# Windowed attention and a PReLU feed-forward layer in one kernel: weights converted earlier, and the first tile's activation split over two slots

## The chip, the cores and the metric

The kernel runs on one core of one Trainium2 chip. The metric is device time in microseconds (us) of one execution; a kernel is run several times and the median counts. Profiles are of single executions taken by the hardware profiler. Engines are named as in the profile: PE multiplies matrices (PEld is its loading of weights), DVE is the vector engine, ACT the scalar (activation) engine, SP the engine that issues the transfers.

## The reference

Inputs are q, k and v of shape (8, 8, 576, 64) (batch, head, position, head dimension), two matrices w_in (512 x 2048) and w_out (2048 x 512), and a vector alpha of 2048. Cut to what matters:

```python
scores = q @ k.T / sqrt(64)          # per batch and head
# heads 0-3: the last 32 positions; heads 4-7: every 4th of the last 128
attn = softmax(where(mask, scores, -1e9))
x = (attn @ v)                       # laid out as 4608 tokens x 512
h = x @ w_in
g = maximum(h, 0) + alpha * minimum(h, 0)
out = g @ w_out
```

## The kernel before, in words

**Work and tiles.** Attention is cut into units `Unit(b, c, u)`: batch b, head pair c (4), half u (2) of the 576 positions; 8 units a batch, 64 in all. A unit has these steps: `load` (L106, issued by SP), `scores` on PE (L124, tile `s`), `maxima` on DVE (L139, mask and row maximum), `exponentials` on ACT (L148), `divisions` on DVE (L155 to L158), `transposes` on PE (L165, tile `t`), `copies` on ACT (L170, tile `pt`), `values` on PE (L177, tile `o`), and `highs` on ACT (L210) and `lows` on DVE (L214), which write the result to `x` as two parts, a rounded high part and the rest. All products of the feed-forward layer are made from such pairs, as three passes (high x high, high x low, low x high).

The feed-forward layer takes the 4608 tokens in 9 tiles of 512 (t) and the 2048 hidden columns in 16 chunks of 128 (f). One (t, f) is a slot here, numbered n = 16 t + f. A slot has `ffn_h` (L259, 12 matmuls into a PSUM tile `h`), `ffn_g` (L264 to L279: PReLU to `m`, then the cast of its high part to `g`, L277), `ffn_low` (L283, low part of `g`), and `ffn_y` (L291, 12 matmuls that add into four PSUM tiles `y`). In the first tile (`begin`) the PReLU goes over ACT: relu of -h to `m` (L269), relu of h to `r` (L270), and one sum on DVE (L271). In the other tiles it is two instructions on DVE (L274, L275).

**Weights.** w_in and w_out arrive as 64-bit floats, in 32 chunks of 512 KB: `load_weight(which, f)` stages one in a buffer of tag "g" (SP, L223 or L225), `convert_weight` makes 32-bit high and low parts of it: an Abs on ACT (L238), four integer and clamping steps on DVE (L239, L240, L242, L244; tile `wa`, tag "m"), a cast on ACT (L246) and a subtraction on DVE (L247). A chunk (0, f) of w_in is needed by h of hidden chunk f, a chunk (1, f) of w_out by y of it. The converted weights stay in SBUF for the other eight tiles.

**Order.** `wq` lists the chunks in the order of their need. Before the first slot comes a loop over 11 steps, which runs the 8 units of batch 0 as a pipeline: scores of unit s, divisions of unit s-1, transposes of s-2, values of s-3. At its steps 3, 5, 7 and 9 it converts one chunk and loads the next; two chunks are staged ahead. Then slots 0 to 143 follow. While `wq` holds chunks, a slot converts two of them, one behind `exponentials` and one behind `lows`: 28 chunks in slots 0 to 13. Batch 1's units start in slots 0, 2, 4, 6, 8, 10, 12 and 13 (scores there, transposes a slot later, values two slots later), so that two slots share one unit. `pending` delays y: by one slot in the first tile, by two later.

**Buffers.** Pool `ffp` has 4 buffers of tag "g" (the two parts of g; staged chunks) and 4 of tag "m" (`m`, `r`, `wa`, the output). PSUM has 4 banks of tag "a" (s, t, o and h) and 4 of tag "y" (y; before the first slot, s of batch 0). `early` is a third room of the x pool and holds the probabilities of batch 0.

**What sets the order on an engine.** The text of the kernel gives priorities. The framework turns it into one fixed list of instructions for each engine, in which an instruction may stand ahead of others that the text has earlier, and adds the waits. On the chip each engine works its list in order.

## Time and profile before

| | us |
|---|---|
| median of 3 runs | 994.12 |
| lowest, highest | 988.69, 994.39 |
| the profiled execution | 995.82 |
| its span, first to last instruction | 993.9 |
| PE, DVE, ACT busy in the span | 964.2, 580.9, 382.9 |

The busy time of an engine is the time in which it has an instruction under way; matmuls are pipelined and their ends are modelled, so a PE that is busy all the time isn't at its peak. PEclk is the clock granted to PE, as tenths or as a share of full speed. In groups a row reads: line, engine, operation, output<-input, count | busy us, mean ns of one | idle time of the engine ahead of it and what ended it. In a list of waits: the engine and line that waited, for whom, us in total, times, longest. In a timeline: start, length, engine, line, operation, count, and in brackets the idle time ahead of it. In a table of stages: from:to, length, then busy us (and instructions) of PE, PEld, DVE, ACT, POOL, then the granted clock, the share of DMA time and GB/s.

### The profile page before, as it was taken

How to read it: one execution, taken by the hardware profiler on the slowest of the kernel's cores; microseconds unless marked ns; L12 is line 12 of the kernel's file. 1: busy time of each engine (PE TensorE's matmuls, PEld its weight loads, DVE VectorE, ACT ScalarE, POOL GpSimd, SP SyncE). 2: the span in 40 equal slices, each digit the busy share in tenths (PEclk: the TensorE clock that was granted, in tenths of full speed). 3: DMA queues.
4: the chain of work that ended last, by engine and by line, in shares of the span. 5: the costliest groups of instructions: out<-in, count | busy, mean ns of one | idle time of the engine just before them, and what ended most of it. 6: DMA issues, size and time to landing. Idle time of an engine off the chain costs nothing.

```text
span 993.9 us, 14724 instructions
## 1 busy us (share of the span) xinstructions
PE 964.2 (97%) x5388; PEld 770.4 (78%) x5388; DVE 580.9 (58%) x1732; ACT 382.9 (39%) x1267; POOL 0.6 (0%) x6
## 2 busy tenths in 40 slices
PE   7699999999999999999999999999999999999998
PEld 4466766788888888888888888888888888888886
DVE  5869899755555556655555556555555544434343
ACT  5757667533433334433343334333433321111111
POOL 0000000000000000000000000000000000000000
PEclk8579899999999999999999999999999999999999
DMA  7334543211112111211121112111121001001001
GB/s 234 116 104 163 164 156 125 83 41 40 41 38 67 33 41 40 83 41 41 41 82 36 32 41 83 41 41 40 41 74 32 1 1 43 1 1 43 0 1 43
DMA packets 39303, 58.78 MB, mean 59 GB/s; under 512 B 3808, under 2 KB 28480, under 8 KB 39232
## 3 DMA queue, kind: packets, MB, share of 16 engines
q1 hardware_dynamic: 39232, 57.84, 18.6%
q8 instruction: 43, 0.70, 0.3%
q14 instruction: 28, 0.23, 0.1%
HBM read 48.39 MB, written 9.44 MB: 58 GB/s over the span
## 4 chain that ended last, share of the span: by engine, by line
PE 88%; DVE 7%; ACT 2%; issue 1%; DMA 1%; SPq 0%; ACTq 0%
PE h L259 38%; PE y L291 37%; PE s L124 5%; PE o L177 4%; PE t L165 3%; DVE wa L244 1%; DVE wa L242 1%; DVE wa L239 1%; DMA q<-qT 1%; DVE pr L139 1%; ACT early L148 1%; DVE wi L247 1%; DVE pr L158 1%; DVE wo L247 1%; DVE m L271 1%
## 5 line engine op out<-in xcount | busy, mean ns | idle before, releaser
L291 PE MATMUL y<-g,wo 128*128 128x512 f32 x1728 | 431.1, 397 | 7.2 <-ACT g L277 7.2
L259 PE MATMUL h<-x,wi 128*128 128x512 f32 x1728 | 427.4, 397 | 0.0
L259 PEld LDWEIGHTS h<-x,wi 128*128 128x128 f32 x1728 | 331.2, 192 | 69.8 <-issue 0.4
L291 PEld LDWEIGHTS y<-g,wo 128*128 128x128 f32 x1728 | 315.8, 188 | 81.4 <-ACT g L277 10.6
L274 DVE TENSOR_SCALAR m<-h,al 128x512 f32<-128x512 f32 x128 | 96.1, 751 | 278.8 <-PE h L259 274.2
L277 ACT CAST g<-m 128x512 fp32r<-128x512 f32 x144 | 89.5, 621 | 188.5 <-DVE m L275 185.8
L283 DVE TENSOR_TENSOR g<-m,g 128x512 fp32r<-128x512 f32 x144 | 99.1, 688 | 55.8 <-ACT g L277 55.6
L148 ACT ACTIVATE pr<-pr,nm 96x128 f32<-96x128 f32 x336 | 130.8, 392 | 2.3 <-DVE nm L139 2.2
L210 ACT CAST x<-o 128x288 fp32r<-128x288 f32 (+8 forms) x112 | 36.0, 393 | 218.3 <-PE o L177 218.3
L170 ACT COPY pt<-t 128x288 f32<-128x288 f32 x128 | 46.2, 400 | 141.7 <-PE t L165 141.2
L275 DVE SCALAR_TENSOR_TENSOR m<-h,m 128x512 f32<-128x512 f32 x128 | 88.5, 692 | 4.4
L139 DVE CUSTOM_DVE_ANT_0 pr<-s,mask_sb 96x128 f32<-96x128 f32 x336 | 75.2, 281 | 0.0
L124 PE MATMUL s<-k,q 64*96 64x128 f32 x768 | 62.2, 290 | 5.1 <-DMA q<-qT 5.1
L148 ACT ACTIVATION_READ_ACCUMULATOR pr<-pr,nm 96x1 f32 x336 | 63.6, 189 | 0.0
L158 DVE TENSOR_TENSOR pr<-pr,rs 96x384 f32<-96x384 f32 x112 | 57.7, 550 | 1.7
L124 PEld LDWEIGHTS s<-k,q 64*96 64x96 f32 x768 | 47.1, 165 | 14.8 <-issue 6.7
L177 PEld LDWEIGHTS o<-pt,v 128*64 128x64 f32 x768 | 37.2, 143 | 23.9 <-issue 20.5
L177 PE MATMUL o<-pt,v 128*64 128x96 f32 x768 | 50.9, 264 | 0.6 <-ACT pt L170 0.2
L165 PEld LDWEIGHTS t<-ident,pr 96*128 96x128 f32 x336 | 34.4, 142 | 15.2 <-DVE pr L158 8.1
L165 PE MATMUL t<-ident,pr 96*128 96x96 f32 x336 | 40.2, 252 | 4.2 <-DVE pr L158 4.1
L214 DVE TENSOR_TENSOR x<-o,x 128x288 fp32r<-128x288 f32 (+8 forms) x112 | 41.4, 383 | 3.7 <-ACT x L210 3.7
L139 DVE DVE_READ_ACCUMULATOR2_ANT nm<- 96x1 f32 x384 | 30.4, 79 | 0.0
(33 smaller groups left out, 281.6 us busy)
## 6 DMA issues: line engine op xcount, KB each, us to landing
v<-vW SPq DMA_DIRECT2D x64, 192.0 KB, 2.3
k<-kT SPq DMA_DIRECT2D x32, 288.0 KB, 3.2
q<-qT SPq DMA_DIRECT2D x64, 144.0 KB, 2.8
out<-ob SPq DMA_DIRECT2D x36, 256.0 KB, 2.2
ws<-w_in SPq DMA_DIRECT2D x16, 512.0 KB, 3.6
ws<-w_out SPq DMA_DIRECT2D x16, 512.0 KB, 3.5
mask_sb<-masks SPq DMA_DIRECT2D x1, 144.0 KB, 3.6
al<-alpha SPq DMA_DIRECT2D x1, 8.0 KB, 3.2
```

Of the source, the lines that this page charges most:

```text
L124: nc.tensor.matmul(self.ps[e][:, i, :], lhsT=self.q[rows, i * BQ:(i + 1) * BQ], rhs=self.k[rows, self.starts[j]:self.starts[j] + P], start ...
L139: nc.vector.tensor_tensor_reduce(out=self.pr[e][:, i, :], in0=self.ps[e][:, i, :], in1=mask_sb[:, self.kinds[j], :], scale=-SCALE, scalar= ...
L148: nc.scalar.activation(out=self.pr[e][:, i, :], in_=self.pr[e][:, i, :], func=AF.Exp, bias=self.nm[:, e, i:i + 1], scale=-1.0, accum_out=s ...
L158: nc.vector.tensor_tensor(out=self.pr[e], in0=self.pr[e], in1=rs[:, e, :, None].broadcast_to([BQ, UB, P]), op=ALU.mult)
L165: nc.tensor.transpose(out=self.tp[e][:, i, :], in_=self.pr[e][:, i, :], identity=ident)
L177: nc.tensor.matmul(self.po[e * D:(e + 1) * D, i, :], lhsT=self.v[:, e, i, :], rhs=self.pt[e][:, i, :], start=True, stop=True,)
L259: nc.tensor.matmul(ps, lhsT=wi[:, a, f, c, :], rhs=x[:, c, e, :], start=(n == 0), stop=(n == 3 * NC - 1))
L274: nc.vector.tensor_scalar(out=m, in0=ps, scalar1=0.0, scalar2=al[:, f:f + 1], op0=ALU.min, op1=ALU.mult)
L275: nc.vector.scalar_tensor_tensor(out=m, in0=ps, scalar=0.0, in1=m, op0=ALU.max, op1=ALU.add)
L277: nc.scalar.copy(out=g[:, 0, :], in_=m)
L283: nc.vector.tensor_tensor(out=g[:, 1, :], in0=ms.pop((t, f)), in1=g[:, 0, :].bitcast(F32), op=ALU.subtract)
L291: nc.tensor.matmul(ys[t][c], lhsT=wo[:, a, f, c * P:(c + 1) * P], rhs=g[:, e, :], start=(f == 0 and n == 0), stop=(f == NF - 1 and n == 2),)
```

## The change

The order of `wq` stays. Four things are edited:

- A function `weight()` converts the next chunk and loads one more. The attention loop calls it at steps 1 to 8, behind `exponentials` and ahead of `lows` and `divisions`, instead of at steps 3, 5, 7 and 9 behind `divisions`. So 8 chunks stand ahead of the first slot and 24 are left for slots 0 to 11.
- Three chunks are loaded ahead of the loop instead of two: the first behind the masks and ahead of the second unit's q and v, the second behind those, the third behind alpha.
- In the first tile `ffn_g` is split. `ffn_relu` issues the two relus, the second now in place in the PSUM tile of h (no tile `r`), late in the slot. `ffn_sum` does the sum and the cast at the head of the next slot, reading the relu of h from PSUM. The first `weight()` of a slot stands right behind that, ahead of `maxima`; `ffn_low`, at its old place, is that of the slot before; the second `weight()` stands behind the relus. y keeps its slot: y of slot n is still issued at the end of slot n+1.
- The other tiles do what they did; the first slot of the second tile also does the sum, cast and low of the last slot of the first.

```diff
-    def ffn_g(t, f, spare_dve):
+    def ffn_relu(t, f):
+
         ps = ms[t, f]
         m = ffp.tile([P, TT], F32, tag="m", name=f"m_{t}_{f}")
-        if spare_dve:
-            r = ffp.tile([P, TT], F32, tag="m", name=f"r_{t}_{f}")
-            nc.scalar.activation(out=m, in_=ps, func=AF.Relu, scale=-1.0)
-            nc.scalar.activation(out=r, in_=ps, func=AF.Relu)
-            nc.vector.scalar_tensor_tensor(
-                out=m, in0=m, scalar=nal[:, f:f + 1], in1=r, op0=ALU.mult, op1=ALU.add)
...
+        nc.scalar.activation(out=m, in_=ps, func=AF.Relu, scale=-1.0)
+        nc.scalar.activation(out=ps, in_=ps, func=AF.Relu)
+        ms[t, f] = ps, m
+
+    def ffn_sum(t, f):
+        ps, m = ms[t, f]
+        nc.vector.scalar_tensor_tensor(
+            out=m, in0=m, scalar=nal[:, f:f + 1], in1=ps, op0=ALU.mult, op1=ALU.add)
+        gs[t, f] = g = ffp.tile([P, 2, TT], F32R, tag="g", name=f"g_{t}_{f}")
+        nc.scalar.copy(out=g[:, 0, :], in_=m)
+        ms[t, f] = m
...
+    loads = list(wq)
+
+    def weight():
+        if wq:
+            convert_weight(*wq.pop(0))
+            if loads:
+                load_weight(*loads.pop(0))
+
...
     nc.sync.dma_start(out=mask_sb, in_=masks)
+    load_weight(*loads.pop(0))
     first[1].load()
+    load_weight(*loads.pop(0))
     nc.sync.dma_start(out=al, in_=alpha)
     nc.vector.tensor_scalar_mul(nal, al, -1.0)
-    loads = list(wq)
-    load_weight(*loads.pop(0))
     load_weight(*loads.pop(0))
...
             u.exponentials()
+        if 1 <= s <= len(first):
+            weight()
         if u := at(3):
             u.lows()
         if u := at(1):
             u.divisions()
-        if s >= 3 and s % 2 and ahead:
-            convert_weight(*wq.pop(0))
-            load_weight(*loads.pop(0))
-            ahead -= 1
...
-        ffn_g(t, f, begin)
+
+        if begin:
+            done = raw
+            for args in done:
+                ffn_sum(*args)
+            weight()
+        else:
+            done = raw + [(t, f)]
+            for args in raw:
+                ffn_sum(*args)
+            ffn_g(t, f)
         for u in score:
             u.maxima()
         for u in value:
             u.highs()
         for u in score:
             u.exponentials()
-        if wq:
-            convert_weight(*wq.pop(0))
-            if loads:
-                load_weight(*loads.pop(0))
-        ffn_low(t, f)
+        for args in done:
+            ffn_low(*args)
         for u in value:
             u.lows()
-        if wq:
-            convert_weight(*wq.pop(0))
-            if loads:
-                load_weight(*loads.pop(0))
+        raw = []
+        if begin:
+            ffn_relu(t, f)
+            raw = [(t, f)]
+            weight()
         for u in score:
             u.divisions()
-        while len(pending) >= lag:
+        if begin:
+            pending += done
+        while len(pending) >= (1 if begin else 2):
             ffn_y(*pending.pop(0))
-        pending.append((t, f))
+        if not begin:
+            pending += done
```

More of the change, by code (lines that the diff above doesn't have):

```diff
@@ L262, in ffn_h, with ffn_g @@
         ms[t, f] = ps
-    def ffn_g(t, f, spare_dve):
+    def ffn_relu(t, f):
         ps = ms[t, f]
         m = ffp.tile([P, TT], F32, tag="m", name=f"m_{t}_{f}")
-        if spare_dve:
-            r = ffp.tile([P, TT], F32, tag="m", name=f"r_{t}_{f}")
-            nc.scalar.activation(out=m, in_=ps, func=AF.Relu, scale=-1.0)
-            nc.scalar.activation(out=r, in_=ps, func=AF.Relu)
-            nc.vector.scalar_tensor_tensor(
-                out=m, in0=m, scalar=nal[:, f:f + 1], in1=r, op0=ALU.mult, op1=ALU.add)
-        else:
-            nc.vector.tensor_scalar(out=m, in0=ps, scalar1=0.0, scalar2=al[:, f:f + 1], op0=ALU.min, op1=ALU.mult)
-            nc.vector.scalar_tensor_tensor(out=m, in0=ps, scalar=0.0, in1=m, op0=ALU.max, op1=ALU.add)
+        nc.scalar.activation(out=m, in_=ps, func=AF.Relu, scale=-1.0)
[8 more added lines that the diff above has]
+        ms[t, f] = m
+    def ffn_g(t, f):
+        ps = ms[t, f]
+        m = ffp.tile([P, TT], F32, tag="m", name=f"m_{t}_{f}")
+        nc.vector.tensor_scalar(out=m, in0=ps, scalar1=0.0, scalar2=al[:, f:f + 1], op0=ALU.min, op1=ALU.mult)
+        nc.vector.scalar_tensor_tensor(out=m, in0=ps, scalar=0.0, in1=m, op0=ALU.max, op1=ALU.add)
         g = ffp.tile([P, 2, TT], F32R, tag="g", name=f"g_{t}_{f}")
@@ L306, in tile_window_attention_prelu_ffn @@
     wq = [(0, 0), (0, 1), (1, 0), (0, 2)]
-    ahead = len(wq)
     for f in range(1, NF):
@@ L368, in tile_window_attention_prelu_ffn @@
             todo[s + 2][3].append(unit)
-    pending = []
+    pending, raw = [], []
     for n in range(NTILE * NF):
@@ L373, in tile_window_attention_prelu_ffn @@
         begin = t == 0
-        lag = 1 if begin else 2
         load, score, trans, value = todo[n]
```

## The prediction

> **What bounds the kernel now.** I read the page's slices first, then a table of stages, then who waited for whom on the engine that came out full.
>
> ```profile
> span 993.9 us, 14724 instructions
> PE   7699999999999999999999999999999999999998
> DVE  5869899755555556655555556555555544434343
> ACT  5757667533433334433343334333433321111111
> PEclk8579899999999999999999999999999999999999
> ```
>
> A slice is 24.8 us. From the ninth on, PE is full at full clock and DVE has a third of its time free: there the change touches nothing that could matter. Only the first eight slices, some 190 us, have gaps on PE, and there DVE is at 8 or 9 tenths. The same stretch as a table of stages (busy us on each engine, then granted clock and DMA share):
>
> ```profile
> 7.80:53.40 45.60, 32.43 (x237) 23.87 (x234) 34.20 (x162) 32.40 (x134) 0.00 (x0) 0.64 0.50 160
> 53.40:74.20 20.80, 18.49 (x90) 13.38 (x90) 15.15 (x41) 12.22 (x31) 0.00 (x0) 0.80 0.34 110
> 74.20:158.50 84.30, 77.34 (x399) 58.63 (x398) 78.63 (x213) 57.71 (x155) 0.00 (x0) 0.92 0.50 160
> 158.50:177.00 18.50, 16.45 (x93) 12.16 (x92) 18.24 (x58) 13.75 (x43) 0.00 (x0) 1.00 0.27 91
> 116.80:133.40 16.60, 15.29 (x81) 11.57 (x79) 15.32 (x44) 10.76 (x31) 0.00 (x0) 0.91 0.45 146
> 206.40:219.60 13.20, 13.20 (x80) 10.67 (x79) 7.18 (x23) 4.72 (x19) 0.00 (x0) 1.00 0.14 39
> ```
>
> The first row is the attention of batch 0 with four chunks of weights, up to the start of the first tile's work; the next three hold the other 28 chunks, two a slot. The fifth is one pair of slots out of that stage (two slots share one attention unit): DVE and PE each work 15.3 of 16.6 us. The last is a pair of the next tile, which PE alone sets at 13.2 us. So conversions cost: a pair with four of them takes 16.6 us where PE needs 13.2. The last chunk ends at 177:
>
> ```profile
> L247 DVE TENSOR_TENSOR wo<-wa,wo x1: 681/681/681, 176.3 to 176.3; 128x512 fp32r<-128x512 f32 x1
> ```
>
> From 7.8 to there DVE works 34.20 + 15.15 + 78.63 + 18.24 = 146.2 us and idles 45.6 + 20.8 + 84.3 + 18.5 - 146.2 = 23.0 us. Where that idle time lies (waits of DVE from 7 to 60 us, then from 60 to 177):
>
> ```profile
> DVE early L139 <- PE s L124: 5.3, 4, 2.9
> DVE x L214 <- ACT x L210: 3.7, 2, 2.6
> DVE m L271 <- ACT r L270: 3.3, 1, 3.3
> DVE wi L247 <- ACT wi L246: 2.2, 1, 2.2
> DVE wa L239 <- ACT wa L238: 0.7, 2, 0.4
> ...
> DVE m L271 <- ACT r L270: 5.3, 5, 2.3
> DVE wi L247 <- ACT wi L246: 2.5, 6, 0.6
> ```
>
> The two waits for r, 8.6 us together, are what the delayed sum aims at; 5.3 us are maxima waiting for scores, 3.7 us the last lows before the first h.
>
> **The change, part by part.** No computing instruction is removed or added: 32 conversions, the same relus, sums, casts and lows. What moves is which work DVE may do while it would idle. So the sum is one of DVE's idle time.
>
> *The price of a conversion.* A group's mean is longer than what an instruction takes from DVE, since neighbours overlap; starts count (start, length):
>
> ```profile
> 100.12 0.68 DVE L247 TENSOR_TENSOR wi<-wa,wi 128x512 fp32r<-128x512 f32 x1
> 100.72 0.68 DVE L242 SCALAR_TENSOR_TENSOR wa<-ws,wa 128x512 uint32<-128x512 uint32 x1
> 101.32 0.42 DVE L239 TENSOR_SCALAR wa<-wa 128x512 f32<-128x512 f32 x1
> 101.66 0.68 DVE L244 SCALAR_TENSOR_TENSOR wa<-ws,wa 128x512 uint32<-128x512 uint32 x1
> 102.26 0.42 DVE L240 TENSOR_SCALAR wa<-wa 128x512 uint32<-128x512 uint32 x1
> ```
>
> L247, L242 and L244 take 0.60 us, L239 and L240 0.34: 2.48 us a chunk. The rows are also out of the text's order (L242 between another chunk's steps): each engine's instructions stand in an order made from the text, not in the text's own, so a chunk that has landed can be taken into a gap.
>
> *Eight chunks instead of four ahead of the first h.* That puts 4 x 2.48 = 9.9 us on DVE into the first row's 45.6 us, which has 11.4 free, and takes two slots' worth of conversions off the end: the last chunk falls in slot 11, not 13. Work before the last chunk then drops by what slots 12 and 13 hold besides conversions, 15.32 - 9.92 = 5.4 us. The last chunk ends at 7.8 + 146.2 - 5.4 + I = 148.6 + I, I being DVE's idle time up to there. Two more slots are then to be done at PE's pace, 13.2 us, before the position of 177 is reached. So the change saves 177 - (148.6 + I + 13.2) = 15.2 - I. It pays only if I falls well below the present 23.0; 7.8 us of the idle time removed only pay for what moved.
>
> *I in the attention stage* (11.4 now). The 5.3 us before scores are time in which a landed chunk can be converted. But one chunk is now issued ahead of the second unit's loads and three ahead of the third's. Its q already lands late behind two chunks (start and length):
>
> ```profile
> 5.59 7.64 DMA q<-qT
> ...
> ws<-w_in SPq DMA_DIRECT2D x4, 512.0 KB, 5.3
> q<-qT SPq DMA_DIRECT2D x12, 144.0 KB, 3.2
> ```
>
> Against a median of 3.2 us it takes 7.64, so two chunks cost some 4.4 us and the third 2.2. SP issues in order, so the key, q and v loads behind it move too. I take 2 us left of 5.3 (bounds 0 and 5.3 + 2.2). The lows' 3.7 us can be filled by chunks 9 and 10, if staged: 1.5 left (0 to 3.7). Waits of a chunk's last step for ACT's cast and of its first for ACT's Abs are 2.9 us with four chunks; eight in the same stretch, on an ACT that is busy 32.4 of 45.6 us and gets another 4 x (Abs + cast): 3.5 (1 to 5.8). Sum 7.
>
> *I from the first h to slot 3* (5.65 now). The sum of slot n stands at the head of slot n+1, so the 3.3 and 2.3 us of waiting for r go. What is late next is the relu behind h(0), for which ACT holds its queue, the next Abs among it. I take 1 (0 to 2.3).
>
> *I in the six pairs of slots 0 to 11* (74.2 to 158.5: 84.3 - 78.63 = 5.7 us over five pairs, 1.1 a pair). DVE needs 15.3 and PE, as it runs there, 15.3 too:
>
> ```profile
> 133.13 0.47 PE L165 MATMUL t<-ident,pr 96*128 96x96 f32 x3 [0.60 <-DVE pr L158]
> 133.38 4.58 PE L259 MATMUL h<-x,wi 128*128 128x512 f32 x12
> 141.31 2.88 PE L259 MATMUL h<-x,wi 128*128 128x512 f32 x12
> 144.03 2.88 PE L291 MATMUL y<-g,wo 128*128 128x512 f32 x12
> ```
>
> The h behind the transposes takes 4.58 us, the other 2.88, like y: after waits of under a us the clock is down (0.91 in that pair). The transposes still wait for the divisions and h still stands behind them. Two engines that need 15.3 each and hang on each other do not reach 15.3; I take 0.7 of idle time a pair, 4.2 (bounds 0.3 and 1.1, the present value: 1.8 to 6.7).
>
> The Trainium skill, "TensorE: Matmul & The Clock Gate", Part 1 (The HAM clock gate), says that the clock halves only after an idle window of about 3.4 us. The trace differs: here it drops with waits below 1 us. By the rule PE would need only 13.2 a pair, DVE alone would be the limit, the pairs' idle time would go to its lower bound and the result would be about 2 us faster than by the rows; I go by the rows.
>
> *The relu in place and the sum from PSUM.* No row shows ACT writing 512 wide into PSUM. The nearest are these (mean ns):
>
> ```profile
> L271 DVE SCALAR_TENSOR_TENSOR m<-m,nal,r 128x512 f32<-128x512 f32 x11 | 8.2, 746 | 5.3 <-ACT r L270 5.3
> L275 DVE SCALAR_TENSOR_TENSOR m<-h,m 128x512 f32<-128x512 f32 x128 | 88.5, 692 | 4.4
> ```
>
> The second already reads one input from PSUM and is 54 ns shorter; over the 11 sums before the last chunk 0.6 us, between 0 and 0.6. ACT has a third of its time free in the tile stage, so a relu dearer or cheaper by a tenth of a us is hidden; without that cover 16 of them cost 1.6.
>
> *Three chunks staged instead of two.* They hold three of the four "g" buffers. It removes waits of ACT for landings:
>
> ```profile
> ACT wa L238 <- DMA ws<-w_in: 5.0, 4, 1.7
> ```
>
> These four waits hide behind DVE's own backlog (DVE waited 0.3 us for an Abs after 60 us): 0. The price on g is the second rival.
>
> *Sum.* I = 7 + 1 + 4.2 = 12.2; saving 15.2 - 12.2 + 0.6 = 3.6 us. The profiled execution took 995.82 us with a span of 993.9; 995.8 - 3.6 = 992.2. The median shown, 994.12, lies 1.7 below that execution, so the forecast for the median is 990.5. The terms' bounds give I from 1 + 0 + 1.8 = 2.8 to 17 + 2.3 + 6.7 = 26, that is 12.4 + 0.6 saved to 10.8 lost, 981 to 1005; the likeliest case is the middle of this, 984 to 999.
>
> **Rivals.**
>
> *DVE's idle time all but goes* (I of 2.8 to 5). For it: every large wait of DVE's list is of a kind that an early chunk or the delayed sum can cover. Against: PE's own 15.3 a pair at the lowered clock, and that covering needs the instruction order to fit real durations. Saving 10.8 to 13, middle 12: 982.
>
> *One g buffer becomes the bound; slower.* With three of four held by staged chunks, the cast of slot n+1 must wait until y of slot n has left its buffer. Per slot: cast, low, y, and on PE, which works in order, an h and half a unit's products. With the rows
>
> ```profile
> L277 ACT CAST g<-m 128x512 fp32r<-128x512 f32 x144 | 89.5, 621 | 188.5 <-DVE m L275 185.8
> L283 DVE TENSOR_TENSOR g<-m,g 128x512 fp32r<-128x512 f32 x144 | 99.1, 688 | 55.8 <-ACT g L277 55.6
> ```
>
> that is 0.62 + 0.69 + 2.88 + 2.88 to 4.58 for h + about 1.1 = 8.2 to 9.9 us, against DVE's 7.7 a slot. It decides once PE runs an h between a low and its y: then a pair takes 16.4 to 19.7 us, middle 18, DVE idles 2.7 a pair, I = 8 + 6 x 2.7 = 24.2, 15.2 - 24.2 + 0.6 = 8.4 lost: 1002.5. Behind a held cast on ACT stand the next Abs and exps, for which DVE waits. Against it: y can be put ahead of that h, which leaves 5.3 us, and the order is free to do so.
>
> *The change doesn't do what it says*: the early chunks land too late (5.3 us median, DMA share 0.5 in the stage) or stand too late in the engines' order, conversions run as now, and only the waits for r go: but they only become the wait for h. Then the last chunk stays near 177, and the time near 994. For it: in the present trace the chunks already run whenever there is room.
>
> **How the numbers follow.** Chances: the forecast 0.52, idle time gone 0.23, one g buffer 0.14, nothing moved 0.11. The predicted time is the forecast's, 990.5. A measurement of this kernel can tell about 1%, 9.9 us: below 984.2 or above 1004.1. Faster takes most of the first rival and a little of the forecast's edge, 0.25; slower most of the second, 0.12; within 1% the rest, 0.63. The range, 981 to 1003, is the span of the terms' bounds, cut to the second rival's middle.
>
> **What would show it.** Right: eight L247 end before the first h's end, the last chunk ends near 160, waits of the sum for a relu below 1 us in all, DVE busy 15.3 of about 16 us a pair, six such pairs and then 13.2 us. The first h, whose present last matmuls are these,
>
> ```profile
> 51.29 4.28 PE L259 MATMUL h<-x,wi 128*128 128x512 f32 x10
> ```
>
> should end later than at 55.6, by 1 to 8 us. Wrong: the last chunk after 170; L277 waiting for "PE y" in most slots of the first tile; scores of the third unit waiting over 5 us more for q; or any difference behind 200 us, where nothing is changed.

## The result and the profile after

The changed kernel takes 998.0 us, median of ten runs (996.71 to 1000.12); the kernel before, run beside it, 988.6 us, median of ten (987.0 to 994.39). The ratio is 1.008, interval 1.0057 to 1.0103: 9.4 us slower, where 3.6 us faster was forecast. The time lies inside the predicted range, but on the other side of the kernel before.

The kernel before needs a word of its own, since everything is measured against it. Its 130 runs in the sessions of this study lie between 984.7 and 996.4 us, 49 of them below 990 and 73 above 991. The clock granted to PE goes with the time: of the 120 runs that were timed beside the experiments, the 43 below 990 us have 0.979 to 0.986, the 69 above 991 us 0.972 to 0.979. The execution that was shown ahead of the prediction, 995.82 us, is one of the long ones. The changed kernel's runs do not spread like that. Against the median of all 130, 992.0, the changed kernel loses 6.0 us; against that of its own session, 9.4.

The page of the changed kernel, its span and slices (24.9 us each):

```profile
span 997.8 us, 14728 instructions
PE   7669899999999999999999999999999999999998
DVE  6879998655555555555555556555555544334343
PEclk7569999999999999999999999999999999999999
```

DVE stands a tenth lower in the seventh and eighth slice: the conversions do end earlier. But the third slice of PE, from 50 to 75 us, is at 6 where it was at 9, and the clock is a tenth lower in the first and the third. As stages (busy us and instructions on PE, PE's weight loads, DVE, ACT, POOL; granted clock, DMA share, GB/s):

```profile
7.80:53.40 45.60, 29.86 (x198) 22.75 (x198) 39.58 (x171) 35.27 (x135) 0.00 (x0) 0.57 0.64 209
53.40:74.20 20.80, 14.31 (x71) 9.96 (x70) 14.21 (x44) 10.61 (x31) 0.00 (x0) 0.66 0.26 84
74.20:158.50 84.30, 76.66 (x411) 58.06 (x410) 79.05 (x212) 56.98 (x151) 0.00 (x0) 0.95 0.47 150
158.50:177.00 18.50, 18.19 (x120) 14.08 (x119) 12.99 (x46) 11.90 (x40) 0.00 (x0) 1.00 0.15 43
```

In the first row DVE does more than before (39.58 us for 34.20), as planned, but PE does less (198 matmuls for 237): the attention of batch 0 has fallen behind. In the second row the first h, which ended at 55.6 before, ends only at 66.0, and DVE is busy for only 14.21 of 20.8 us. The fourth is what was wanted, PE nearly alone. The last chunk and the waits of DVE from 60 to 190 us:

```profile
L247 DVE TENSOR_TENSOR wo<-wa,wo x2: 683/684/686, 158.4 to 162.6; 128x512 fp32r<-128x512 f32 x2
```

```profile
DVE m L274 <- ACT h L269: 12.7, 7, 4.2
DVE x L214 <- ACT x L210: 3.1, 2, 2.7
```

The last chunk ends at 163.3 (before: 177). The sum still waits for a relu: what was a wait for r is now a wait for the relu in place (tile h, L269). Of the 12.7 us, 4.8 lie ahead of the end of the last chunk; the rest lies where PE is full and DVE's idle time costs nothing. The prediction's sign was below 1 us. The first h's last matmuls and the first y:

```profile
62.13 3.85 PE L259 MATMUL h<-x,wi 128*128 128x512 f32 x10
...
73.60 0.79 PE L300 MATMUL y<-g,wo 128*128 128x512 f32 x1 [3.84 <-ACT g L277]
```

The first h ends at 66.0, not at 55.6. The end of the 17th h, the first of the next tile, is at 189.4 (before: 185.3), and from there to the span's end it is 808.4 us here and 808.6 before. So the whole difference lies ahead of 190 us, where it was looked for.

### The profile page after: what moved, and what is told of

Its sections match the earlier page's. It is cut to its first block, busy times and chain, and to the rows that moved or that the text cites. A ratio compares the mean times of both kernels' runs of the same rounds, so it can differ in the third digit from the quotient of the medians.

```text
span 997.8 us, 14728 instructions
## 1 busy us (share of the span) xinstructions
PE 962.3 (96%) x5388; PEld 770.2 (77%) x5388; DVE 581.6 (58%) x1732; ACT 382.6 (38%) x1267; POOL 0.6 (0%) x6
## 4 chain that ended last, share of the span: by engine, by line
PE 90%; DVE 3%; ACT 3%; DMA 2%; issue 1%; SPq 0%; ACTq 0%
PE y L300 40%; PE h L259 38%; PE s L124 4%; PE o L177 4%; PE t L165 3%; DMA ws<-w_out 1%; ACT pr L148 1%; DMA q<-qT 1%; ACT wa L238 1%; ACT early L148 0%; DVE wa L242 0%; DVE early L158 0%; DVE m L274 0%; DVE wa L244 0%; ACT m L268 0%
## 5 line engine op out<-in xcount | busy, mean ns | idle before, releaser
L259 PE MATMUL h<-x,wi 128*128 128x512 f32 x1728 | 421.5, 392 | 1.7 <-DVE m L274 1.5
L259 PEld LDWEIGHTS h<-x,wi 128*128 128x128 f32 x1728 | 325.3, 189 | 70.6 <-DVE m L274 2.1
L283 DVE TENSOR_SCALAR m<-h,al 128x512 f32<-128x512 f32 x128 | 96.1, 751 | 279.5 <-PE h L259 274.9
L286 ACT CAST g<-m 128x512 fp32r<-128x512 f32 x128 | 79.5, 621 | 186.5 <-DVE m L284 185.9
L292 DVE TENSOR_TENSOR g<-m,g 128x512 fp32r<-128x512 f32 x144 | 99.0, 688 | 55.8 <-ACT g L286 55.6
L139 DVE CUSTOM_DVE_ANT_0 pr<-s,mask_sb 96x128 f32<-96x128 f32 x336 | 75.0, 281 | 0.0
L177 PE MATMUL o<-pt,v 128*64 128x96 f32 x768 | 53.5, 270 | 0.7 <-ACT pt L170 0.5
L139 DVE DVE_READ_ACCUMULATOR2_ANT nm<- 96x1 f32 x384 | 30.2, 79 | 0.0
```

The source lines that it names most:

```text
L139: nc.vector.tensor_tensor_reduce(out=self.pr[e][:, i, :], in0=self.ps[e][:, i, :], in1=mask_sb[:, self.kinds[j], :], scale=-SCALE, scalar= ...
L177: nc.tensor.matmul(self.po[e * D:(e + 1) * D, i, :], lhsT=self.v[:, e, i, :], rhs=self.pt[e][:, i, :], start=True, stop=True,)
L259: nc.tensor.matmul(ps, lhsT=wi[:, a, f, c, :], rhs=x[:, c, e, :], start=(n == 0), stop=(n == 3 * NC - 1))
L283: nc.vector.tensor_scalar(out=m, in0=ps, scalar1=0.0, scalar2=al[:, f:f + 1], op0=ALU.min, op1=ALU.mult)
L286: nc.scalar.copy(out=g[:, 0, :], in_=m)
L292: nc.vector.tensor_tensor(out=g[:, 1, :], in0=ms.pop((t, f)), in1=g[:, 0, :].bitcast(F32), op=ALU.subtract)
```

## The experiments

After the result there were two theories. One: the attention stage of batch 0 has no DVE time to give; what is put there delays the first h by as much, and a chunk costs more there than in the slots. The rival: the loss comes from the slots of the first tile (here the tile stage), from the delayed sum, the relus in place, or from windows of lowered clock. A third reading, that DVE's total work is the bound so that any work taken off it helps, came in on the way. The table gives, of each profiled run, the end of the first h, the end of the 17th, and the span; behind the 17th h all have 808.3 to 809.4 us left.

| kernel | first h | 17th h | span |
|---|---|---|---|
| before, as shown | 55.6 | 185.3 | 993.9 |
| before, second execution | 53.9 | 176.2 | 984.8 |
| the change | 66.0 | 189.4 | 997.8 |
| the change, second execution | 66.3 | 189.8 | 998.2 |
| e1, weights only | 63.6 | 192.3 | 1000.6 |
| e2, relus only | 54.4 | 180.4 | 988.8 |
| e3, chunk behind the divisions | 61.7 | 187.9 | 996.3 |
| e5, two chunks ahead | 52.5 | 180.2 | 988.8 |
| e6, six ahead | 60.7 | 184.2 | 992.6 |
| e6 again | 56.3 | 179.8 | 988.2 |
| e7, three staged | 57.2 | 190.4 | 999.2 |
| e8, light chunks | 57.1 | 180.4 | 988.8 |
| e9, last step on POOL | 52.8 | 185.3 | 993.7 |
| e10, the change, last step on POOL | 61.8 | 188.3 | 996.7 |
| e11, relu in place only | 54.2 | 179.2 | 988.0 |
| e12, two ahead, last step on POOL | 48.7 | 180.3 | 989.6 |
| e13, PE filled in batch 1 | 54.2 | 184.4 | 993.5 |
| e14, PE filled in batches 0 and 1 | 52.0 | 179.3 | 987.7 |
| e15, two ahead and PE filled | 46.6 | 175.3 | 983.8 |
| e16, the change, PE filled | 65.2 | 189.6 | 998.0 |

One profile is one execution, and the kernel before shows how far two of them can be apart (9.1 us), so the verdicts on times rest on the medians. Each ratio is to the kernel before in the same session, whose median went from 988.6 to 993.7 us between sessions.

### The change in halves

The weights' half alone: the kernel before with the loads ahead of the first scores and a chunk in each of the steps 1 to 8; its slots and its relus stay.

```
+    load_weight(*loads.pop(0))
     first[1].load()
+    load_weight(*loads.pop(0))
...
+        if 1 <= s <= len(first):
+            weight()
...
-        if s >= 3 and s % 2 and ahead:
-            convert_weight(*wq.pop(0))
-            load_weight(*loads.pop(0))
-            ahead -= 1
```

> The early weights alone (three chunks staged, eight converted in the attention loop), with the activation of the first tile as before. Theory A: the loss arises in the attention stage, where eight chunks on DVE and the waits of a fixed order put the first h 10 us later, and the tile stage gives only some of it back. Then the first h ends near 66 us and the time is as slow as with the whole change, 996 to 999. Theory B (rival): the split of the activation costs the tile stage (the bank of h and the g buffer are held longer), and without it the 9.9 us of the four chunks that left the tile stage come back in full: 987 to 991.

Measured: 1001.94 us (999.1 to 1003.5, six runs), ratio 1.0116, interval 1.0083 to 1.0148, to 989.76 before: 12.2 us slower, no less than the whole change. In its profile the first h ends at 63.6, and from there to the 17th h it takes 192.3 - 63.6 = 128.7 us, where the change takes 123.4.

The relus' half alone: weights as before, relu in place directly behind h, sum a slot later.

```
+        nc.scalar.activation(out=m, in_=ps, func=AF.Relu, scale=-1.0)
+        nc.scalar.activation(out=ps, in_=ps, func=AF.Relu)
+        ms[t, f] = ps, m
...
+            done = raw
+            for args in done:
+                ffn_sum(*args)
+            weight()
```

> The split activation alone, with the weights as before (two chunks staged, four converted in the attention loop, 28 in slots 0 to 13). Theory A: the first h ends near 55.6 us as before, the tile stage is as long or 1 to 3 us shorter: 985 to 989. Theory B: the tile stage becomes longer by 4 to 8 us although nothing moved in the attention stage: 992 to 997.

Measured: 992.89 us (989.77 to 995.88, twelve runs), ratio 1.0033 (1.001 to 1.0056): 3.1 us slower. So neither half brings what it was meant to, and the larger loss comes with the weights.

To see which part of the relus' half costs, e11 has only the relu in place, without the delay:

```
-            r = ffp.tile([P, TT], F32, tag="m", name=f"r_{t}_{f}")
...
-            nc.scalar.activation(out=r, in_=ps, func=AF.Relu)
+            nc.scalar.activation(out=ps, in_=ps, func=AF.Relu)
```

> The kernel before with the second relu written in place into the PSUM tile of h (no r), the sum in the same slot and nothing delayed. It parts the two halves of the split activation, which alone made it 0.33% slower. If holding the bank of h until the sum is what costs: 992 to 994, as with the split alone. If the delay by a slot costs (cast and y of the first slots come later, PE waits and its clock falls): no difference from before, within 0.2%.

Measured: 994.02 us (989.88 to 996.59), ratio 1.0008 (0.999 to 1.0025). No difference: the relu in place and reading the sum from PSUM cost and bring nothing that can be measured. That leaves the delay, and the new order around it, for what e2 loses; but the two intervals overlap, so this is not shown.

### The kernel before, once more

> The kernel before, unchanged, for a second profile: its runs lie in two groups, near 988 and near 994, and the profile at hand is of the later group. Both theories: the two groups part in the first 190 us; a run near 988 has its last conversion 5 to 6 us ahead of 177, or its first h ahead of 55.6.

One execution, 986.75 us, span 984.8. Its stretches from the start of work to the first h's end, on to the last chunk's end, and on to the 17th h's end; first in the execution that the prediction was read from:

```profile
7.80:55.60 47.80, 34.63 (x244) 25.34 (x242) 34.25 (x162) 32.40 (x134) 0.00 (x0) 0.64 0.48 153
55.60:177.00 121.40, 110.07 (x572) 82.69 (x573) 111.97 (x309) 83.68 (x225) 0.00 (x0) 0.92 0.45 144
177.00:185.30 8.30, 8.30 (x55) 6.39 (x55) 5.06 (x22) 4.61 (x17) 0.00 (x0) 1.00 0.16 44
```

then in the second execution:

```profile
7.80:53.90 46.10, 33.72 (x246) 24.83 (x244) 34.26 (x162) 32.29 (x134) 0.00 (x0) 0.67 0.51 161
53.90:167.90 114.00, 101.19 (x572) 75.85 (x573) 111.36 (x309) 82.99 (x225) 0.00 (x0) 1.00 0.48 153
167.90:176.20 8.30, 8.30 (x55) 6.40 (x55) 5.06 (x22) 4.61 (x17) 0.00 (x0) 1.00 0.16 42
```

then in the changed kernel:

```profile
7.80:66.00 58.20, 39.80 (x242) 29.51 (x244) 46.73 (x188) 38.67 (x144) 0.00 (x0) 0.56 0.59 191
66.00:163.30 97.30, 85.83 (x473) 64.91 (x474) 90.88 (x245) 67.30 (x179) 0.00 (x0) 0.95 0.42 134
163.30:189.40 26.10, 25.79 (x155) 20.34 (x154) 14.55 (x61) 14.67 (x54) 0.00 (x0) 1.00 0.16 44
```

These nine rows are the heart of the case. The two executions of the kernel before run the same instructions (309 on DVE and 572 on PE in the second stretch), yet the second stretch takes 121.4 us in one and 114.0 in the other; DVE idles 121.40 - 111.97 = 9.4 us in the first and 114.00 - 111.36 = 2.6 in the second. The clock is 0.92 and 1.00. The waits of DVE for r in that stretch, shown execution, then the second one:

```profile
DVE m L271 <- ACT r L270: 8.6, 6, 3.3
```

```profile
DVE m L271 <- ACT r L270: 2.0, 1, 2.0
```

So most of the 8.6 us that the delayed sum was to win is absent in the execution whose clock stays up. That it goes with h at half clock is read from these two executions. The windows of half clock in the shown execution:

```profile
113.07:116.48 3.41, 1.80 (x9) 1.05 (x9) 3.08 (x8) 2.23 (x4) 0.00 (x0) 1.00 0.44 142
116.48:119.89 3.41, 3.41 (x10) 2.77 (x11) 3.38 (x8) 1.28 (x4) 0.00 (x0) 0.50 0.44 151
130.13:133.54 3.41, 2.10 (x12) 1.37 (x12) 3.41 (x10) 1.75 (x5) 0.00 (x0) 1.00 0.41 138
133.54:136.95 3.41, 3.41 (x10) 2.67 (x10) 3.37 (x7) 1.36 (x3) 0.00 (x0) 0.50 0.44 154
```

The first and third rows are windows at full clock in which PE was busy for 1.80 and 2.10 of 3.41 us, between its waits; the second and fourth, right behind them, are at half clock throughout. The second execution in the first two of these stretches:

```profile
113.07:116.48 3.41, 3.41 (x33) 2.55 (x32) 3.38 (x7) 2.86 (x7) 0.00 (x0) 1.00 0.44 137
116.48:119.89 3.41, 3.41 (x16) 2.82 (x15) 3.41 (x19) 3.41 (x15) 0.00 (x0) 1.00 0.71 240
```

PE is full in both and the clock stays. But it also stays behind this window of the second execution, in which PE was no busier:

```profile
137.12:140.53 3.41, 1.74 (x9) 1.12 (x8) 3.41 (x10) 1.93 (x4) 0.00 (x0) 1.00 0.41 118
140.53:143.95 3.42, 2.81 (x16) 1.94 (x15) 3.42 (x8) 1.77 (x4) 0.00 (x0) 1.00 0.34 94
```

So a half-busy window can be followed by half clock and need not be; what decides is not shown. The windows of the shown execution lie 133.54 - 116.48 = 17.06 us apart, five times 3.41, and a pair of slots there takes as long (ends of every second h at 104.2, 121.2, 138.0 and 155.0). The same distance stands in the first profile of e6, whose windows from 117.05, 134.12 and 151.19 on are at half clock.

The Trainium skill, "TensorE: Matmul & The Clock Gate", Part 1 (The HAM clock gate), describes a free-running window of 3413 ns, and a clock that halves after an idle window. The length agrees with these rows. The condition does not: here windows that were half busy were followed by half clock, 1.80 and 2.10 us of 3.41. The prediction weighed the rule against the rows and kept the rows. That was right for the shown execution; in the second one the clock stays at 1.00 for the whole stretch and DVE is the limit, as the prediction had it for the rule. What was missed is that both occur.

### Where in the attention stage

e3 is the changed kernel with its chunk behind the divisions of the step.

```
-        if 1 <= s <= len(first):
-            weight()
         if u := at(3):
             u.lows()
         if u := at(1):
             u.divisions()
+        if 1 <= s <= len(first):
+            weight()
```

> The whole change, but the attention loop has each of its eight conversions behind the divisions instead of ahead of lows and divisions. Theory A, with the place in the order as its cause: the divisions and with them transposes and values come earlier, the first h ends 3 to 6 us sooner than at 66 and the time is 992 to 996. If the work of eight chunks in that stage is the cause and not their place, the first h stays within 2 us of 66 and the time at 996 to 999. Theory B expects the last, too.

Measured: 995.82 us (994.44 to 998.05, nine runs), ratio 1.006 (1.0035 to 1.0084) to 989.76. The first h comes 4.3 us earlier than in the changed kernel (61.7), the time is not clearly better (its interval overlaps that of the change). Of the 4.3 us only 1.5 are left at the end of the 17th h (187.9 for 189.4). The place within the step is at most a part of the loss.

e7 is the kernel before with the changed kernel's order of loads (three chunks staged) and still four conversions ahead.

```
+    loads = list(wq)
     nc.sync.dma_start(out=mask_sb, in_=masks)
+    load_weight(*loads.pop(0))
     first[1].load()
+    load_weight(*loads.pop(0))
```

> The kernel before with three chunks staged in the changed order of loads (one ahead of the second unit's, one behind, one behind alpha), four converted as before. Theory C: the third unit's q lands up to 2 us later, the first h ends 0 to 2 us behind 53.9, time 989 to 992. Rival (the loads in front of the units explain the longer attention stage): first h at 60 or later, 995 or more.

Measured: 994.58 us (988.19 to 1000.93, twelve runs), ratio 1.0028 (1.0001 to 1.0056) to 992.43. The loads are not free, though only just beyond the noise. Where it shows is the start, alike in e7 and in the changed kernel; the first matmuls of scores of the kernel before, then of the changed kernel (start, length, idle time before):

```profile
6.69 1.81 PE L124 MATMUL s<-k,q 64*96 64x128 f32 x24
13.36 0.96 PE L124 MATMUL s<-k,q 64*96 64x128 f32 x6 [4.86 <-DMA q<-qT]
```

```profile
6.69 0.98 PE L124 MATMUL s<-k,q 64*96 64x128 f32 x12
9.24 0.90 PE L124 MATMUL s<-k,q 64*96 64x128 f32 x12 [1.56 <-DMA q<-qT]
13.78 0.53 PE L124 MATMUL s<-k,q 64*96 64x128 f32 x2 [3.64 <-DMA q<-qT]
```

Before, the scores of the first two units run as one; now the second unit waits for its q, behind a chunk of 512 KB. The third unit's, which the prediction had feared for, are only 0.4 us later. In e7 the first h ends at 57.2, 1.6 to 3.3 us later than in the two executions of before. Its profiled execution is its slowest, 1000.93 us, and loses more in the tile stage.

e8 takes work away instead of moving it: the changed kernel, with the four DVE steps L239 to L244 left out for the chunks of steps 5 to 8. Their Abs, casts, last step and loads stay.

```
-        if 1 <= s <= len(first):
-            weight()
+        if 1 <= s <= len(first):
+            weight(s > 4)
```

> The whole change, with the four integer and clamping steps on DVE left out for the chunks that are converted at steps 5 to 8 (Abs, cast and subtraction stay; these weights are not converted rightly). That takes 4 x 1.88 = 7.5 us off DVE in the attention stage and nothing else. Theory C, the price being DVE's work: the first h ends at 58 to 61 instead of 66, time 989 to 993. Rival (ACT's order or the landing of chunks sets the stage): first h at 64 or later, time 996 to 998.

Measured: 989.77 us (988.55 to 992.47, twelve runs), ratio 0.9969 (0.9951 to 0.9987) to 992.43. That is 8.2 us below the changed kernel's 998.0 (another session), for 4 x (2.48 - 0.60) = 7.5 us of DVE's work less. The rest of this kernel is the changed one. Up to its first h:

```profile
7.80:57.10 49.30, 37.70 (x242) 28.75 (x244) 38.95 (x170) 37.87 (x144) 0.00 (x0) 0.58 0.68 225
```

DVE has 46.73 - 38.95 = 7.8 us less to do there and the first h ends 8.9 us earlier, at 57.1; DVE's idle time, 49.30 - 38.95 = 10.4, is much as in the changed kernel (58.20 - 46.73 = 11.5), and the same number of chunks still lands and passes ACT. The 17th h ends 9.0 us earlier. This is the run that decides: most of the loss is DVE's work ahead of the first h, here about us for us to the very end, and the work on ACT, which stays, is not its cause. What is left, 57.1 for 53.9 or 55.6 before, is what e7 has with the loads alone (57.2). The casts of the four chunks then wait for no step of DVE either; that was not tried apart from the work.

Why DVE's idle time there cannot be used shows in PE's waits up to the first h, changed kernel:

```profile
PE t L165 <- DVE early L158: 12.5, 7, 2.9
```

and in the second execution of the kernel before:

```profile
PE t L165 <- DVE early L158: 7.2, 5, 3.1
```

PE waits for DVE's divisions for 7.2 us already before the change, and for 12.5 after it; in between DVE waits for PE's scores. It is a chain of the two engines (scores, maxima, divisions, transposes, values, lows). My reading, which no run tests by itself, is that DVE's gaps stand where PE works and a chunk's steps, once begun there, run into the next divisions.

### How many chunks ahead

e5 converts two ahead of the first h, e6 six; nothing else differs from the kernel before.

```
-        if s >= 3 and s % 2 and ahead:
+        if s in (3, 7):
```

```
-        if s >= 3 and s % 2 and ahead:
+        if 3 <= s <= 8:
```

> The kernel before with two chunks converted in the attention loop (steps 3 and 7) instead of four, 30 in the slots. Theory C (rate of exchange): in undisturbed runs of before a pair of slots already takes what DVE works in it, 15.4 us, where PE needs 13.2, so a chunk in the tile stage costs 0.55 us, while in the attention stage it costs up to its 2.48 us of DVE. Two chunks fewer there: the first h ends 2 to 5 us ahead of 53.9, the tile stage is 1 to 2 us longer, the time is 985 to 989 against some 989.8 of before. Rival (the first four chunks fit into idle time of the attention stage at no cost): first h at 53 to 54.5, time 991 to 993.

> The kernel before with six chunks converted in the attention loop (steps 3 to 8), still two staged, still behind the divisions. Theory C: the first h ends 3 to 5 us behind 53.9, the tile stage is 1 us shorter, time 992 to 995. Rival (not the number of chunks but the early loads and the place ahead of the divisions made the attention stage longer): first h within 1.5 us of 53.9, time 987 to 990.

Measured: e5 990.59 us (985.23 to 992.15), ratio 0.9973 (0.9949 to 0.9998); e6 992.61 us (985.6 to 994.88), ratio 0.9989 (0.9964 to 1.0015); twelve runs each, before 992.43. Fewer is a little better; six is not measurably worse than four, which the theory had not expected. Its profile had shown the first h at 60.7, with everything from 30 us on shifted by some 4 us, so it was profiled again, and the change too:

> The kernel with six chunks in the attention loop, for a second profile. If each early chunk is paid steadily: the first h ends at 59 to 61 again. If not: 55 to 58, with a time near 986 to 988.

> The changed kernel, unchanged, for a second profile. If the attention stage pays steadily: the first h ends at 64.5 to 66.5 us again and DVE's work before it is 46 to 47 us. If the lateness changes with the clock from run to run: outside of 64 to 67.

Measured: e6 again 989.99 us with the first h at 56.3; the change again 999.99 us with the first h at 66.3. The change's lateness is steady, that of e6 was not. DVE from the start to the first h's end, with two, six (second profile) and eight chunks behind the divisions (e3, which has the changed kernel's loads too):

```profile
7.80:52.50 44.70, 34.98 (x230) 25.86 (x230) 28.84 (x148) 29.88 (x130) 0.00 (x0) 0.66 0.45 141
```

```profile
7.80:56.30 48.50, 33.10 (x240) 24.35 (x236) 38.92 (x172) 34.47 (x138) 0.00 (x0) 0.68 0.54 172
```

```profile
7.80:61.70 53.90, 34.27 (x246) 25.06 (x246) 45.12 (x181) 37.63 (x143) 0.00 (x0) 0.68 0.59 195
```

DVE's idle time is 44.70 - 28.84 = 15.9, 48.50 - 38.92 = 9.6 and 53.90 - 45.12 = 8.8 us, with 11.8 for four (second execution) and 11.5 in the change. But these executions start differently. In the profile of e5 and the first of e6 PE waits 5.7 and 6.0 us for the third unit's q, and the first chunk is done at 30.4 and 30.7; in the second of e6 and the second of before it waits 4.3 and 3.9 us, and the chunk is done at 26.9 and 27.6. Like with like, from two to six chunks the first h comes 60.7 - 52.5 = 8.2 us later for 38.49 - 28.84 = 9.7 of work, and from four to six 56.3 - 53.9 = 2.4 us for 38.92 - 34.26 = 4.7. So a chunk there costs between half and nearly all of its work; whether the stage takes the first ones more cheaply than the last is not shown. Why the change as it stands is 4.3 us later still than e3 (place in the step, the chunks of steps 1 and 2, the load that delays the second unit) was not told apart.

### DVE's work moved to POOL

If DVE's total were the bound, its 0.60 us for the last step of each chunk could go to POOL, which is idle.

```
-        nc.vector.tensor_tensor(out=dst[:, 1, :], in0=af, in1=dst[:, 0, :].bitcast(F32), op=ALU.subtract)
+        nc.gpsimd.tensor_tensor(out=dst[:, 1, :], in0=af, in1=dst[:, 0, :].bitcast(F32), op=ALU.subtract)
```

e9 does this to the kernel before, e10 to the changed one, e12 to e5.

> The kernel before with the last step of each conversion, the subtraction of L247, on POOL, which is busy 0.6 us in the whole span. Theory C (DVE's work per chunk is what the stage pays): 0.60 us a chunk leave DVE, 28 x 0.6 = 17 us in the slots, of which at most 2.2 us a pair count before PE sets the pair at 13.2: up to 7 pairs x 2.2 = 15 us, and 0 to 2 us ahead of the first h. Expected 978 to 985 against some 990 of before. Rival (the pairs hang on the round of waits between PE, ACT and DVE and not on DVE's work, or POOL and DVE slow each other down): 988 or more.

> The whole change with the same subtraction on POOL. Theory C: 8 x 0.6 = 4.8 us less on DVE ahead of the first h, which ends at 61 to 63 instead of 66, and tile pairs down to 13.5 to 14.5 us; 984 to 991 against 998 of the whole change. Rival: 995 or more.

> Two chunks instead of four in the attention loop, with the subtraction on POOL: the candidate that the runs point to. Theory C: first h 1 to 2 us ahead of before's, pairs as with the subtraction on POOL, two more chunks in the slots: within 2 us of that kernel, 977 to 985. Rival: 987 or more.

Measured, twelve runs each, before 993.69: e9 995.48 us (992.71 to 997.33), ratio 1.0031 (1.0012 to 1.0051); e10 997.14 (996.21 to 998.73), 1.0041 (1.0024 to 1.0058); e12 992.73 (991.4 to 998.09), 1.0018 (0.9993 to 1.0043). A clear miss: with all 32 last steps gone from DVE, e9 is slower. Its groups on POOL (60 to 170 us; busy us, mean ns) and then on DVE (74 to 160 us):

```profile
L247 POOL TENSOR_TENSOR wo<-wa,wo 128x512 fp32r<-128x512 f32 x13 | 20.5, 1574 | 50.7 <-ACT wo L246 50.7
```

```profile
L242 DVE SCALAR_TENSOR_TENSOR wa<-ws,wa 128x512 uint32<-128x512 uint32 x21 | 17.4, 831 | 0.2
L239 DVE TENSOR_SCALAR wa<-wa 128x512 f32<-128x512 f32 x21 | 13.2, 629 | 0.0
```

The same groups on DVE of the kernel before (second execution):

```profile
L242 DVE SCALAR_TENSOR_TENSOR wa<-ws,wa 128x512 uint32<-128x512 uint32 x22 | 15.0, 683 | 0.2
L239 DVE TENSOR_SCALAR wa<-wa 128x512 f32<-128x512 f32 x22 | 9.0, 411 | 0.1
```

One of e9's subtractions and the L242 that meets it (start, length):

```profile
93.78 1.27 POOL L247 TENSOR_TENSOR wo<-wa,wo 128x512 fp32r<-128x512 f32 x1 [3.58 <-ACT wo L246]
93.89 1.71 DVE L242 SCALAR_TENSOR_TENSOR wa<-ws,wa 128x512 uint32<-128x512 uint32 x1
```

Two more lines of DVE in e9 (shortest/median/longest in ns, first and last start), L283 from 60 to 165 us and L139 from 74 to 160:

```profile
L283 DVE TENSOR_TENSOR g<-m,g x12: 678/680/1761, 64.6 to 158.5; 128x512 fp32r<-128x512 f32 x12
L139 DVE CUSTOM_DVE_ANT_0 pr<-s,mask_sb x30: 275/278/281, 88.7 to 157.2; 96x128 f32<-96x128 f32 x30
```

The subtraction takes POOL 1574 ns, as far as spans on POOL can be read, instead of DVE's 680, and the mean of DVE's own L242 goes from 683 to 831 ns and that of L239 from 411 to 629. The means mix two cases. An L242 or L239 that meets a subtraction on POOL can take up to 1720 or 1519 ns, about 1 us more than alone; the others take what they took. The L283 that meets one, at 64.58, takes 1761 ns; between 74 and 160 us none does, and there it takes 678 to 694. L139 meets many and keeps its 280. DVE stays full, 83.39 of 84.30 us between 74.2 and 158.5. In e10 the first h does end at 61.8, 4.2 us earlier than in the change, as expected, though DVE is busy for as long ahead of it (46.63 us); from there to the 17th h it takes 126.5 us for 123.4, so little is left at the end. The third reading is not refuted by this, since DVE got no lighter; but this way is closed.

The Trainium skill, "GPSIMD Engine Reference", 1. Specifications, says that POOL shares its SBUF interfaces with DVE and contends with DVE instructions in a two-port mode or with two inputs in SBUF. The trace agrees: L242 and L283 have both inputs in SBUF and become longer where they meet POOL, L139 has one of its two in PSUM and does not. L239 has one input; whether it runs in a two-port mode no run here shows. The price is the runs': up to about 1 us for an instruction that meets a subtraction.

### The clock's gaps filled

e13 is the kernel before with zero products on PE ahead of each unit's transposes in the tile stage (batch 1), where PE waits for the divisions; they write to the PSUM tile that the transposes then overwrite, ten of 128x288 a unit.

```
             for e in range(2):
+                for i in range(5 if self.b == 1 else 0):
+                    nc.tensor.matmul(
+                        self.tp[e], lhsT=calm, rhs=calm[:, None, :BQ].broadcast_to([P, UB, BQ]), start=True, stop=True)
```

e14 has them in batch 0 too (`self.b <= 1`), e15 is e14 with two chunks ahead as in e5, e16 is the changed kernel with e13's.

> The kernel before with ten products of zeros (128 x 288, bf16) on PE ahead of the transposes of each of batch 1's eight units, written to the tiles that the transposes then overwrite. Theory D (before's two groups are half-clock windows that recur with the pairs, because PE waits in each pair): the waits are filled, no half-clock window between 80 and 165 us, all runs in the lower group, 985 to 989 median. Rival (the groups have another cause, and the fillers cost PE time): 992 or more, in two groups still or above both.

> The same with fillers ahead of the transposes of batch 0's units too. Theory D: the attention stage, whose transposes, values and first h run at half clock, gains 1 to 4 us on top: first h at 50 to 53, 982 to 988. Rival: the fillers stand in front of the transposes on a PE that works in order, the first h comes 1 to 5 us later than 54 to 55.6: 990 to 996.

> The same fillers with two chunks in the attention loop instead of four. Theory D with the price of an early chunk: 0 to 3 us less than the run with four chunks and the same fillers. Rival: no difference or more, within 1 us.

> The whole change with the fillers in batch 1's units. With the windows gone on both sides the change is to be seen without them: the first h still 10 to 12 us later, the tile stage 2 to 4 us shorter than that of the kernel before with fillers, 994 to 998, some 8 us above it. Rival (the change's loss is one of clock windows): within 3 us of the kernel before with fillers.

Measured, before 991.58 (29 runs): e13 994.97 us (993.39 to 1000.03, twelve), ratio 1.0045 (1.002 to 1.0069); e14 989.41 (987.33 to 992.62, twelve), 0.9988 (0.9968 to 1.0007); e15 985.9 (984.03 to 988.5, twelve), 0.9948 (0.9927 to 0.9969); e16 1000.3 (998.73 to 1001.19, six), 1.009 (1.0058 to 1.0121).

e13 is a miss that teaches. Its stages:

```profile
52.00:99.40 47.40, 47.31 (x275) 36.92 (x274) 43.72 (x122) 34.41 (x90) 0.00 (x0) 1.00 0.47 151
99.40:150.00 50.60, 48.81 (x275) 37.86 (x275) 47.34 (x128) 35.77 (x91) 0.00 (x0) 1.00 0.50 158
150.00:170.00 20.00, 17.42 (x85) 12.82 (x86) 17.42 (x56) 13.02 (x40) 0.00 (x0) 0.83 0.37 119
```

The clock is at 1.00 up to 150 us, as meant. But the products take PE's time ahead of the rest, and DVE idles 47.40 - 43.72 = 3.7 us in the first row, where it idles 2.6 in the whole stretch of before's second execution; in the last row the clock is at 0.83. Full clock is not full speed. In e16 the changed kernel's tile stage runs at 0.98 instead of 0.95 and its time is no better; it is 5.3 us above e13, where the rival had at most 3. So the change's loss is not mainly one of clock there. How much of it is stays open, since the products cost time of their own, as e13 shows. Of the rival's other parts e11 clears the relu in place, and the delayed sum alone costs the 3.1 us of e2; the weights alone lose 12.2, so it is not what makes the change slow.

In the attention stage the clock does count, as e15's rows up to its first h and from there to its 17th show:

```profile
7.80:46.60 38.80, 33.23 (x324) 24.85 (x322) 29.52 (x152) 29.64 (x130) 0.00 (x0) 0.96 0.51 161
46.60:175.30 128.70, 122.37 (x705) 91.40 (x706) 121.39 (x339) 91.29 (x246) 0.00 (x0) 0.99 0.46 147
```

With the clock at 0.96 instead of e5's 0.66, DVE's idle time is 38.80 - 29.52 = 9.3 us instead of 15.9 and the first h is out at 46.6 instead of 52.5. These are single executions, and e5's is one with the late q; with four chunks the first h is at 52.0 with the products (e14) and at 53.9 and 55.6 without. e15 is faster than both kernels, by 0.5% against the one before, and its twelve runs keep within 4.5 us where those of the kernel before, in the same session, spread over 10.3.

## Why the prediction was wrong

The prediction's sum can be put as: gained is the fall of DVE's idle time up to the last chunk, lost is the price of moving two slots' work. It had (23.0 - 12.2) - (13.2 - 5.4) + 0.6 = 3.6 us gained. The nine rows above give the same terms as measured. The move's price is 26.10 - 8.30 = 17.8 us more behind the last chunk, less the DVE work that went from ahead of it, 34.25 + 111.97 - 46.73 - 90.88 = 8.6: 9.2. Idle time after is 58.20 - 46.73 + 97.30 - 90.88 = 17.9. Against the shown execution (23.0 - 17.9) - 9.2 = 4.1 lost, which is 189.4 - 185.3. Against the second, where idle time was 46.10 - 34.26 + 114.00 - 111.36 = 14.5 and the work 145.6, it is (14.5 - 17.9) - (17.8 - 8.0) = 13.2 lost, 189.4 - 176.2. The medians' 9.4 lies between.

- *The base, 23.0 us of idle time: the step that failed first.* It came from one execution, and 8.5 us of it are absent in another execution of the same kernel, whose clock stays at 1.00 behind the first h. With 14.5 as base, even the predicted I of 12.2 leaves 2.3 gained, and 7.8 - 0.6 to pay: 4.9 slower. The shown time, 995.82, above all of 988.69 to 994.39, was the hint.
- *I in the attention stage, 7: too low by 4.5, the largest miss within one execution.* Up to the first h's end it was 11.5, against 11.8 in the second execution of before: nothing was filled. That most of the 5.3 us of waits for scores and of the 3.7 for lows can be filled was the assumption; they are one side of a chain in which PE waits for DVE as well. In e8 the work of four chunks there, taken off DVE, comes back at the end about us for us. The first h came 10.4 to 12.1 us later, for 1 to 8 predicted.
- *I in the tile stage, 1 + 4.2: too low by 1.2.* It was 97.30 - 90.88 = 6.4. That the waits for r only become waits for h had been given to the rival in which nothing moves; it holds in the change too, 4.8 us up to the last chunk where below 1 was the sign.
- *The price of the move, 13.2 for 5.4: too low by 1.4 in the shown execution.* Behind the last chunk PE has 155 matmuls to do where it had 55, 25.79 us of work; the pairs at the end of the first tile are not yet the next tile's 13.2.
- *The sum from PSUM, 0.6:* nothing (e11). In the changed kernel a sum takes 743 ns, as before:

```profile
L274 DVE SCALAR_TENSOR_TENSOR m<-m,nal,h 128x512 f32<-128x512 f32 x13 | 9.7, 743 | 5.0 <-ACT h L269 4.8
```

- *Three staged chunks at 0:* wrong in place. They cost at the second unit's q, not at g or at the third unit's; with their order of loads alone e7 is 0.3% slower.

One reading of the slices was loose as well: DVE is not at 8 or 9 tenths in all of the first eight slices, it is at 5, 6 and 7 in the first, the third and the eighth. The sum did not use it.

Together 4.5 + 1.2 + 1.4 + 0.6 = 7.7 us, the way from 3.6 gained to 4.1 lost; the rest to the medians' 9.4 is the base.

Right were: the last chunk near 160 (163.3), eight conversions ahead of the first h (there are nine), DVE's 2.48 us a chunk (46.73 - 34.25 = 12.5 for five more), and that nothing changes behind 200 us. The rival with one g buffer fell: ACT's cast waited for a y once, 0.3 us. The slower outcome came, but by the attention stage, which had been given no rival of its own; it had been counted as a place with 11.4 us free. The terms were there to see it: a chunk taken out of a slot saves (16.6 - 13.2) / 4 = 0.85 us by the shown execution, and one put ahead of the first h costs up to its 2.48.

Open: why the medians show no price for six chunks ahead (e6) and a large one for eight; how much of the move's price is DVE's work, how much its place ahead of the divisions and how much the loads; and the spread of the kernel before, which goes with the granted clock in its runs, and for which the windows of half clock behind the first h are seen in the long and not in the short profiled execution, but whose onset was not tried by itself. In e13, which took most of the windows away, the gain did not come.

## What to carry to other kernels

Idle time of an engine in a stage where two engines wait for each other in turn is not free time: before work is moved into it, ask who waits for that engine there, and price the move at up to its full length unless an experiment shows less. A wait read from a profile is a base only if a second execution shows it too; where the runs of one kernel spread by more than the expected gain, compare a long and a short one first, the granted clock above all. And price a piece of work in both places: here 0.85 us where it was and up to 2.48 where it went.

## What the hardware showed that was not expected

Windows of 3.41 us of half clock follow windows in which PE was busy for 1.80 to 2.10 us, not only idle ones, and they came 17.06 us apart in a loop of about that period; but a window with 1.74 us of work was followed by full clock in another execution. Zero products ahead of the transposes hold the clock up: in the attention stage 0.96 instead of 0.66 (e15 and e5). A DVE instruction that meets a 128x512 subtraction on POOL can take about 1 us longer (1.71 us for 0.68 in L242, 1.76 for 0.68 in L283), unless, like L139 here, it has an input in PSUM; and the subtraction itself takes POOL 1574 ns for DVE's 680.
